# Narrow experts: fewer background steps, the decode last, half sums in other tiles; branch hints moved and added; the last expert's third block turned earlier

## The chip, the core and the metric

The kernel runs on one core of a Trainium2 chip. The metric is the device time of the slowest core in microseconds (us); the kernel before takes 634.35 us (median of 3 runs, 633.63 to 634.43). TensorE (PE) multiplies, VectorE (DVE) and ScalarE (ACT) work on tiles, GpSimd (POOL) and SyncE (SP) issue transfers here. Each engine runs its own instructions in order and waits on semaphores of the others.

## What is computed

Three layers on 2 sequences of 768 tokens with 512 features: attention of 8 heads (8 global tokens and a window of 96), a layer of 8 experts, and a Fourier mixing with a channel network. The change is in the experts:

```python
for s in range(S):
    fresh_e = argmax(logits[b, s])
    e = fresh_e if s == 0 or local_gate[b, s] < 0.5 else prev_e
    prev_e = e
    h = np.maximum(x[b, s] @ w1[e], 0.0)     # 512 -> 1024
    out[b, s] = p[e] * (h @ w2[e])           # 1024 -> 512
```

Every token goes to one expert, by data. With these inputs the experts 0 to 7 have 324, 177, 166, 172, 115, 206, 96 and 280 tokens.

## The kernel before

After attention and routing, `Moe.run` takes the experts e0 to e7 one after the other (from 127 to 321 us of the profile), each in blocks of 128 tokens that are gathered by index. Products are made in pairs of a high and a low part of each fp32 operand, so that a product of 512 by 1024 is 12 matmuls for each half of 512 columns.

`expert` branches on the number of blocks. Experts with two blocks go through `wide()`: `first256` for the first product (four quarters of 24 matmuls, each into one of two buffers of `ps_h`, read by `hh` on ScalarE and `hl` on VectorE), `third()`, which is a branch on n > 2, and `result` for the second product of each block. An expert with one block goes through `narrow()`: `first128` makes the first product with the tokens stationary, in two half sums; each is copied to SBUF (L1259), turned back by four transposes into `xtp` (L1243), and split into `hh` (L1245, ScalarE) and `hl` (L1246, VectorE). e4 and e6 are narrow here, e1, e2, e3 and e5 wide with `third` skipped. The last expert, e7, is done by sequence: a first block, the third block (taken here), then the second; inside its third block stands a further branch, `rest`, for more than three blocks (not taken here).

Beside the matmuls runs a background of generators. `bg.step(n)` advances each of them n times; `first128` and `second` call the step after every third matmul; `bg.drain()` runs them to the end. The order in which these calls come is the order of the instructions on ScalarE and VectorE. The background of expert e has three things. It converts the four weight pieces of expert e+1 (`Ring.take` on "e"): each is 1024 KB in one of four raw buffers, cast in two halves by ScalarE (L1048, tiles `wide`, `sl0h`, `sl1h`, `sl5h`) with its low parts by VectorE (L1050); when the piece is done, the load of the piece four places on is issued on SP's queue (L986). In experts 0 to 5 it decodes one or two pieces of the later layer ("d": L1081 on ScalarE, then L1090 to L1096 on VectorE, in a tile "dec" of which there are two; the result is written out by POOL, L1014). And `tokens(e + 1)` turns and splits the next expert's tokens (L1164, L1167, L1168). In narrow experts a "dec" tile also holds each half sum.

`mark_branch_hint_location` (L1344) puts a hint for TensorE ahead of the branch of the next expert.

Of the kernel before, what the change touches and what calls it, by code (L numbers as in the profile page):

```python
# [11 lines left out]
F32 = mybir.dt.float32  # L12
# [11 lines left out]
P = 128  # L24
B, H, S, D = 2, 8, 768, 64
E, F = 8, 1024
DM = H * D
# [9 lines left out]
LAST = E - 1  # L37
# [635 lines left out]
TOKENS = 4  # L673
# [253 lines left out]
def rows(st, g):  # L927

    n = 2 if g % 4 < 2 else 4
    out = []  # L930
    for j in range(2):
        hi, lo = (t.rearrange("p (k n) -> p k n", k=n) for t in st.ring.get("e", g + j))
        out += [(hi[:, k], lo[:, k]) for k in range(n)]
    return out
# [165 lines left out]
class Moe:  # L1100
# [81 lines left out]
    def write(self, y, p, d, name="more", beside=None):  # L1182

        nc = self.tc.nc
        ys = self.work.tile([P, DM], F32, name=name, bufs=2 if name == "ys" else 1)
        nc.scalar.activation(ys, y, AF.Copy, scale=p)
        self.scatter(ys, d, beside)
# [43 lines left out]
    def first128(self, w1, x, h, acc, turn, step=lambda: None, hs=None):  # L1231
# [8 lines left out]
        def turned(u):  # L1240
            tp = turn[0].tile([P, 4, P], F32, name=turn[1])
            for k in range(4):
                T.transpose(tp[:, k], hs[u][:, k * P:(k + 1) * P], self.st.ident)  # L1243
            o = slice(4 * u, 4 * u + 4)
            A.activation(hh[:, o], tp, AF.Relu)  # L1245
            V.scalar_tensor_tensor(hl[:, o], tp, 0.0, hh[:, o].bitcast(F32), op0=ALU.max, op1=ALU.subtract)  # L1246
# [12 lines left out]
            A.copy(hs[u], ps)  # L1259
        return lambda: turned(1)  # L1260

    def expert(self, e, n, more, ahead=None):
        tc, ring = self.tc, self.st.ring
        pc, ent = self.pc[e % 2], self.ent[e % 4]
        w1, w2 = rows(self.st, 4 * e), rows(self.st, 4 * e + 2)
        bg = Background()

        def chain(*gs):
            for g in gs:
                yield from g  # L1270


        at = 0 if e else 1
        step = lambda: bg.step(2)
        spare = self.ps_more, "more"

        def result(c, h, y, ys, *more):
            y = self.second(*h, w2, *y, *more)
            bg.drain()
            last = e == LAST and c == 1  # L1280
            write = lambda: self.write(y, pc[:, c:c + 1], ent[:, c, 1:2], ys, "first" if last else None)
            if last:
                self.finish = write
            else:
                write()

        def third():
            self.weight(e, (2,))

            with tc.If(n > 2):  # L1290
                for _ in self.turn(2, 0, self.place(e, 2)):
                    pass
                if e == LAST:
                    self.rest(more)
                late = self.first128(w1, *self.more, spare, spare)
                result(2, self.more[1], spare, "more", lambda: None, late)

        def pieces():
            for units in ring.plan[e]:
                for kind, m in units:  # L1300
                    if kind == "d":
                        ring.begun.pop(ring.at[kind, m], None)
            return ([ring.take(*u, follow=e < LAST) for u in units] for units in ring.plan[e])

        own = lambda s, c: [t[:, :, c * P:(c + 1) * P] for t in s]
        first, then = pieces()

        def wide():
            bg.add(chain(*first))
            calls = iter(range(8))  # L1310
            self.first256(e, lambda: bg.step(2) if e or next(calls) > 1 else None)
            bg.drain()
            if e:
                third()
            bg.add(self.tokens(e + 1))
            bg.add(chain(*then))
            hs = self.hh[0], self.hl[0]
            result(at, own(hs, 0), (self.ps_y, "y"), "ys", step)
            if e:
                result(1, own(hs, 1), spare, "more")  # L1320
            else:
                with tc.If(n > at + 1):
                    result(at + 1, own(hs, 1), spare, "more")

        def narrow():
            first, then = pieces()
            bg.add(chain(*first))
            h = own((self.hh[0], self.hl[0]), 0)
            late = self.first128(w1, own((self.xh[e % 2], self.xl[e % 2]), 0), h, (self.ps_h, "h"), (self.ps_x, "xtp"), step)
            bg.drain()  # L1330
            bg.add(chain(*then))
            calls = iter(range(8))

            def behind():
                if next(calls) == TOKENS:
                    bg.add(self.tokens(e + 1))
                bg.step(2)

            result(0, h, (self.ps_y, "y"), "ys", behind, late)

        if e < LAST:
            if e + 2 < E:
                self.entries(e + 2)
                tc.mark_branch_hint_location(f"wide{e + 1}", hint=(ahead > 1), engines=[mybir.EngineType.PE])  # L1344
            if e == 0:
                wide()
                return
            with tc.If(n > 1, label=f"wide{e}") as arm:
                wide()
            with arm.Else():  # L1350
                narrow()
            return

        for c in range(2):
            x, h = (own(s, c) for s in ((self.xh[e % 2], self.xl[e % 2]), (self.hh[0], self.hl[0])))
            late = self.first128(w1, x, h, (self.ps_h, "h"), (self.ps_x, "xtp"), step, [x[:, :DM] for x in self.xg[:2]])
            if c == 0:
                third()
                bg.add(chain(*first))
            result(c, h, (self.ps_y, "y"), "ys", step, late)  # L1360
            if c == 0:
                self.fetch(0)
# [9 lines left out]
    def rest(self, more):  # L1372

        tc, st, io = self.tc, self.st, self.io
        nc = tc.nc
        A, V = nc.scalar, nc.vector

        def fetch(e, j):
            for u in range(2):
                hi, lo = st.ring.get("e", 4 * (LAST - 1) + 2 + u)  # L1380
                for c in range(0, PW, 1024):
                    cs = slice(c, c + 1024)
                    t = self.st.ring.work.tile([P, PW // 2], F32, name="dec")
                    nc.sync.dma_start(t, io["we"][bass.ds(e * 4 + j + u, 1), :, cs].rearrange("o p n -> (o p) n"))
                    A.copy(hi[:, cs], t)
                    V.tensor_tensor(lo[:, cs], t, hi[:, cs].bitcast(F32), op=ALU.subtract)

        def rows(n):
            out = []
            for u in range(2):  # L1390
                hi, lo = (t.rearrange("p (k n) -> p k n", k=n) for t in st.ring.get("e", 4 * (LAST - 1) + 2 + u))
                out += [(hi[:, k], lo[:, k]) for k in range(n)]
            return out

        with tc.If(more > 0):
            x = self.place(LAST - 1, 2)

            with tc.For_i(0, E + 1, 1) as i:
                n = nc.values_load(st.nch[0:1, bass.ds(i, 1)], min_val=0, max_val=NC)
                e = nc.s_assert_within(i - (i >> 3), 0, LAST, skip_runtime_bounds_check_because="8 becomes 7, the others stay")  # L1400
                first = e * LIST + (i >> 3) * S - ((e + 1) >> 3) * (P + P // 2) + 1
                with tc.For_i(L3, NC, 1) as c:
                    with tc.If(n > c):
                        row = nc.s_assert_within(first + c * P, 0, E * LIST, skip_runtime_bounds_check_because="the row is in the list")
                        p = self.work.tile([P, 1], F32, name="p")
                        o = self.work.tile([P, 2], I32, name="o")
                        nc.sync.dma_start(o, st.list[bass.ds(row, P)])
                        self.gather(x, st.xs, o[:, 0:1])
                        V.tensor_copy(p, x[:, bass.ds(e + DM, 1)])
                        fetch(e, 0)  # L1410
                        s = (LAST - 1) % 2
                        for _ in self.turn(s, 0, x):
                            pass
                        self.first128(rows(2), (self.xh[s][:, :, :P], self.xl[s][:, :, :P]), self.more[1], (self.ps_more, "more"), (self.ps_more, "more"))()
                        fetch(e, 2)
                        y = self.second(*self.more[1], rows(4), self.ps_more, "more")
                        self.write(y, p, o[:, 1:2])
# [522 lines left out]
```

## Time and profile before

| | |
|---|---|
| median of 3 runs | 634.35 us |
| the profiled execution | 635.4 us |
| its span in the profile | 633.6 us |
| TensorE busy | 609.5 us (96%) |
| VectorE, ScalarE, GpSimd busy | 383.8, 275.3, 100.5 us |
| mean granted clock of TensorE | 0.992 |

Times below are us from the start of the span. A row of a timeline gives start, length, engine, line and operation, output and input, shape, count, and in brackets the idle time before it with what released it. The granted clock is TensorE's, as a share of full speed.

### The profile page before, as it was taken

The numbers are of one execution on the slowest core, as the hardware profiler recorded it, in microseconds if no ns is written. First come the engines' busy times: TensorE is split into PE (matmuls) and PEld (weight loads), VectorE is DVE, ScalarE is ACT, GpSimd is POOL, SyncE is SP. The second block draws the span as 40 slices with busy tenths as digits, with TensorE's granted clock in tenths as the row PEclk, the third lists the DMA queues.
The fourth block names the chain that finished last, engine by engine and source line by source line (L and its number), as shares of the span: only waits on it lengthen the run. The fifth ranks groups of instructions, "written<-read, shape, count | busy, mean of one in ns | idle before, by whom it ended". The sixth has DMA issues, their size and how long they took to land.

```text
span 633.6 us, 9722 instructions
## 1 busy us (share of the span) xinstructions
PE 609.5 (96%) x3506; PEld 494.1 (78%) x3507; DVE 383.8 (61%) x898; ACT 275.3 (43%) x548; POOL 100.5 (16%) x147
## 2 busy tenths in 40 slices
PE   9999998799999969898999999999999999999997
PEld 4777875499899849687867887888888888888885
DVE  5778786279786968661389987997531221272112
ACT  5789883266475556552434533441121221131010
POOL 2146662315313312300100000000000000000000
PEclk9999999999999989989999999999999999999999
DMA  8568762279978989961260242551100100100001
GB/s 278 187 204 203 201 120 68 49 283 337 372 250 278 335 288 327 339 210 66 87 250 32 95 173 92 187 190 63 67 0 1 32 36 0 67 2 0 1 0 66
DMA packets 25192, 92.49 MB, mean 146 GB/s; under 512 B 7645, under 2 KB 8797, under 8 KB 17185
## 3 DMA queue, kind: packets, MB, share of 16 engines
q1 hardware_dynamic: 19664, 79.50, 37.6%
q0 software_dynamic: 4736, 10.56, 4.6%
q10 hardware_dynamic: 720, 1.55, 0.7%
q8 instruction: 36, 0.59, 0.4%
q14 instruction: 36, 0.29, 0.2%
HBM read 81.00 MB, written 14.84 MB: 151 GB/s over the span
## 4 chain that ended last, share of the span: by engine, by line
PE 52%; DVE 1%; ACT 0%; issue 0%; DVEq 0%; ACTq 0%
PE h L1742 21%; PE acc L1757 7%; PE acc L1756 7%; PE acc L1758 7%; PE y L1204 1%; PE acc L1576 1%; PE acc L1562 1%; PE more L1254 1%; PE h L1254 1%; PE more L1204 1%; PE f L1708 1%; PE f L1605 1%; PE h L50 1%; PE f L1627 0%; DVE u L1767 0%; PE acc L1565 0%
## 5 line engine op out<-in xcount | busy, mean ns | idle before, releaser
L1747 DVE SCALAR_TENSOR_TENSOR hl<-h,hh 128x512 fp32r<-128x512 f32 x48 | 33.1, 689 | 117.5 <-ACT hh L1746 117.5
L1746 ACT ACTIVATE hh<-h 128x512 fp32r<-128x512 f32 x48 | 28.8, 600 | 164.3 <-PE h L1742 164.3
L1050 DVE TENSOR_TENSOR wide<-raws,wide 128x1024 fp32r<-128x1024 f32 (+1 forms) x38 | 44.8, 1201 | 24.4 <-ACT wide L1048 24.4
L168 ACT ACTIVATE t<-t,nm 128x256 f32<-128x256 f32 (+1 forms) x96 | 46.0, 480 | 10.7 <-DVE nm L159 9.9
L1742 PE MATMUL h<-un0h,wide 128*128 128x512 f32 (+1 forms) x136 | 42.4, 378 | 0.1
L1048 ACT CAST wide<-raws 128x1024 fp32r<-128x1024 f32 (+2 forms) x42 | 40.6, 993 | 4.1 <-PE acc L1758 3.4
L159 DVE CUSTOM_DVE_ANT_0 t<-sp,bias 128x256 f32<-128x256 f32 (+1 forms) x96 | 32.8, 398 | 8.3 <-PE sp L150 4.4
L1757 PE MATMUL acc<-wide,hh 128*128 128x512 f32 x96 | 37.8, 393 | 0.0
L1756 PE MATMUL acc<-wide,hh 128*128 128x512 f32 x96 | 37.6, 392 | 0.0
L1758 PE MATMUL acc<-wide,hl 128*128 128x512 f32 x96 | 37.5, 390 | 0.0
L1133 POOL DMA_INDIRECT xg<-xs,ent x23 | 28.7, 1250 | 39.9 <-PE y L1204 17.4
L1742 PEld LDWEIGHTS h<-un0h,wide 128*128 128x128 f32 x136 | 25.0, 188 | 5.0 <-ACT un0h L1517 0.3
L178 PE MATMUL tp<-consts,t 128*128 128x128 f32 x176 | 26.1, 283 | 1.7 <-ACT p L184 1.7
L178 PEld LDWEIGHTS tp<-consts,t 128*128 128x128 f32 x176 | 18.9, 141 | 9.3 <-ACT p L184 4.9
L1742 PE MATMUL h<-un0l,wide 128*128 128x512 f32 (+1 forms) x68 | 25.6, 377 | 0.0
L192 PE MATMUL sm<-p,vs 128*64 128x128 f32 x352 | 24.5, 279 | 0.0
L184 ACT COPY p<-tp 128x512 f32<-128x512 f32 (+1 forms) x48 | 24.3, 537 | 0.3 <-PE tp L178 0.3
L1081 ACT ACTIVATE dec<-raws 128x1024 f32<-128x1024 f32 x18 | 20.6, 1143 | 4.8 <-issue 4.8
L1224 PE MATMUL h<-xh,wide 128*128 128x256 f32 x160 | 22.5, 279 | 0.0
L1096 DVE SCALAR_TENSOR_TENSOR dec<-raws,dec 128x1024 int32<-128x1024 int32 x18 | 22.0, 1225 | 0.6
L1094 DVE SCALAR_TENSOR_TENSOR dec<-raws,dec 128x1024 int32<-128x1024 int32 x18 | 22.0, 1222 | 0.4
L192 PEld LDWEIGHTS sm<-p,vs 128*64 128x64 f32 x352 | 18.7, 136 | 3.8 <-issue 3.8
(474 smaller groups left out, 1602.3 us busy)
## 6 DMA issues: line engine op xcount, KB each, us to landing
raws<-we SPq DMA_DIRECT2D x31, 1024.0 KB
raws<-wm SPq DMA_DIRECT2D x18, 1024.0 KB
raws<-wmf SPq DMA_DIRECT2D x7, 1024.0 KB
wmf<-dec POOLq DMA_DIRECT2D x8, 512.0 KB
xs<-xrow SPq DMA_DIRECT2D x12, 260.0 KB
vs<-v SPq DMA_DIRECT2D x6, 512.0 KB
raws<-kq SPq DMA_DIRECT2D x3, 1024.0 KB
u<-x SPq DMA_DIRECT2D x6, 512.0 KB
```

The costliest lines, as they stand in the source:

```text
L159: V.tensor_tensor_reduce(out=u.t[:, x, :u.W], in0=u.sp[:, j, k, :u.W], in1=bias[:, 4 * u.g + x, u.b0:u.b0 + u.W], scale=-0.125, scalar=3.0 ...
L168: A.activation(u.t[:, x, :u.W], u.t[:, x, :u.W], AF.Exp, bias=u.nm[:, x:x + 1], scale=-1.0, accum_out=u.den[:, x])
L178: T.transpose(u.tp[k][:, j, c], u.t[:, 2 * k + j, c * P:(c + 1) * P], st.ident)
L192: T.matmul(turned[j * D:j * D + D, k], vs[:, ti % KS, u.h + 2 * k + j], u.p[:, 2 * k + j, c], start=c == 0, stop=c == len(tiles) - 1)
L1048: (first or nc.scalar.copy)(hi[:, cs], raw[:, cs])
L1050: (eng() if callable(eng) else eng or nc.vector).tensor_tensor(lo[:, cs], raw[:, cs], hi[:, cs].bitcast(F32), op=ALU.subtract)
L1742: nc.tensor.matmul(ps[:, c], a[:, k], x[:, k, c], start=n == 0, stop=n == 11)
L1746: nc.scalar.activation(hh, ps, AF.Relu)
L1747: nc.vector.scalar_tensor_tensor(hl, ps, 0.0, hh.bitcast(F32), op0=ALU.max, op1=ALU.subtract)
L1756: T.matmul(acc[c], hh[:, cs], h2, start=first, stop=False)
L1757: T.matmul(acc[c], hh[:, cs], l2, start=False, stop=False)
L1758: T.matmul(acc[c], hl[:, cs], h2, start=False, stop=last)
```

## The change

In `narrow`, a call of the step advances the background once, not twice; in the first product only the first two weight pieces are in it, in the second the other two, until after some steps `tokens(e + 1)` takes their place; what is left of them and the decode come after the result. The half sums go into the tile of the unused third block (`xg2` in e4 and e6) and into a tile `ys`. The hint of the next expert moves from the start of `expert` into `tell()`: after the first block's result in `wide`, after the first product in `narrow`. New hints stand for `third` at the start of `wide` and of e7, and for `rest` in e7's third block. In e7 the third block's tokens are turned in the background of the first block's first product, and `rest` moves behind the third block's result.

```diff
--- before.py
+++ after.py
@@ -1259,6 +1259,9 @@
             A.copy(hs[u], ps)
         return lambda: turned(1)
 
+    def hint(self, label, stay):
+        self.tc.mark_branch_hint_location(label, hint=stay, engines=[mybir.EngineType.PE])
+
     def expert(self, e, n, more, ahead=None):
         tc, ring = self.tc, self.st.ring
         pc, ent = self.pc[e % 2], self.ent[e % 4]
@@ -1287,13 +1290,16 @@
         def third():
             self.weight(e, (2,))
 
-            with tc.If(n > 2):
-                for _ in self.turn(2, 0, self.place(e, 2)):
-                    pass
+            with tc.If(n > 2, label=f"third{e}"):
+                if e < LAST:
+                    for _ in self.turn(2, 0, self.place(e, 2)):
+                        pass
+                else:
+                    self.hint("rest", more > 0)
+                late = self.first128(w1, *self.more, spare, spare)
+                result(2, self.more[1], spare, "more", lambda: None, late)
                 if e == LAST:
                     self.rest(more)
-                late = self.first128(w1, *self.more, spare, spare)
-                result(2, self.more[1], spare, "more", lambda: None, late)
 
         def pieces():
             for units in ring.plan[e]:
@@ -1305,7 +1311,13 @@
         own = lambda s, c: [t[:, :, c * P:(c + 1) * P] for t in s]
         first, then = pieces()
 
+        def tell():
+            if e + 2 < E:
+                self.hint(f"wide{e + 1}", ahead > 1)
+
         def wide():
+            if e:
+                self.hint(f"third{e}", n > 2)
             bg.add(chain(*first))
             calls = iter(range(8))
             self.first256(e, lambda: bg.step(2) if e or next(calls) > 1 else None)
@@ -1316,6 +1328,7 @@
             bg.add(chain(*then))
             hs = self.hh[0], self.hl[0]
             result(at, own(hs, 0), (self.ps_y, "y"), "ys", step)
+            tell()
             if e:
                 result(1, own(hs, 1), spare, "more")
             else:
@@ -1323,25 +1336,36 @@
                     result(at + 1, own(hs, 1), spare, "more")
 
         def narrow():
-            first, then = pieces()
-            bg.add(chain(*first))
+            units = [u for part in ring.plan[e] for u in part]
+            for u in units:
+                if u[0] == "d":
+                    ring.begun.pop(ring.at[u], None)
+            takes = {u: ring.take(*u) for u in units}
+            d = [takes[u] for u in units if u[0] == "d"]
+            bg.add(chain(*(takes["e", 4 * e + 4 + k] for k in range(2))))
             h = own((self.hh[0], self.hl[0]), 0)
-            late = self.first128(w1, own((self.xh[e % 2], self.xl[e % 2]), 0), h, (self.ps_h, "h"), (self.ps_x, "xtp"), step)
+            late = self.first128(w1, own((self.xh[e % 2], self.xl[e % 2]), 0), h, (self.ps_h, "h"), (self.ps_x, "xtp"), bg.step,
+                                 [self.place(e, 2)[:, :DM], self.work.tile([P, DM], F32, name="ys", bufs=2)])
             bg.drain()
-            bg.add(chain(*then))
+            tell()
+            then = chain(*(takes["e", 4 * e + 6 + k] for k in range(2)))
+            bg.add(then)
             calls = iter(range(8))
 
             def behind():
-                if next(calls) == TOKENS:
+                k = next(calls)
+                if k == TOKENS:
+                    bg.live.remove(then)
                     bg.add(self.tokens(e + 1))
-                bg.step(2)
+                bg.step()
 
             result(0, h, (self.ps_y, "y"), "ys", behind, late)
+            bg.add(chain(then, *d))
+            bg.drain()
 
         if e < LAST:
             if e + 2 < E:
                 self.entries(e + 2)
-                tc.mark_branch_hint_location(f"wide{e + 1}", hint=(ahead > 1), engines=[mybir.EngineType.PE])
             if e == 0:
                 wide()
                 return
@@ -1351,6 +1375,8 @@
                 narrow()
             return
 
+        self.hint(f"third{e}", n > 2)
+        bg.add(self.turn(2, 0, self.place(e, 2)))
         for c in range(2):
             x, h = (own(s, c) for s in ((self.xh[e % 2], self.xl[e % 2]), (self.hh[0], self.hl[0])))
             late = self.first128(w1, x, h, (self.ps_h, "h"), (self.ps_x, "xtp"), step, [x[:, :DM] for x in self.xg[:2]])
@@ -1392,7 +1418,7 @@
                 out += [(hi[:, k], lo[:, k]) for k in range(n)]
             return out
 
-        with tc.If(more > 0):
+        with tc.If(more > 0, label="rest"):
             x = self.place(LAST - 1, 2)
 
             with tc.For_i(0, E + 1, 1) as i:
```

Where it moves instructions, before and after. On ScalarE, in e4 from its first product on, before (`raws` is a loaded piece, `h` a half sum in PSUM, `dec` a decode tile):

```order
L1048 CAST wide_106<-raws_63 128x1024 x4
L1259 COPY dec_8489<-h_8490 128x512
L1081 ACTIVATE dec_8518<-raws_63 128x1024
L1245 ACTIVATE hh256_6327<-xtp_8525 128x4x128
L1259 COPY dec_8489<-h_8513 128x512
```

And after:

```order
L1048 CAST wide_106<-raws_63 128x1024 x2
L1259 COPY xg2_6353<-h_8523 128x512
L1048 CAST wide_106<-raws_63 128x1024
L1245 ACTIVATE hh256_6327<-xtp_8550 128x4x128
L1048 CAST wide_106<-raws_63 128x1024
L1259 COPY ys_8522<-h_8541 128x512
```

Two casts stand ahead of the first copy instead of four, and the decode's start (L1081) is gone from between the copy and `hh`.

On VectorE, from the end of e4 into e5, before (the branch is that between the two experts):

```order
L1050 TENSOR_TENSOR sl5l_6319<-raws_63,sl5h_6318 128x1024 x2
L1168 TENSOR_TENSOR xl1_6349<-xtp_8576,xh1_6346 128x4x128
L1168 TENSOR_TENSOR xl1_6349<-xtp_8586,xh1_6346 128x4x128
L1180 COPY pc_6331<-xg0_6351 128x1
L1180 COPY pc_6331<-xg1_6352 128x1
L1348 UNCONDITIONAL_BRANCH
L1348 REGISTER_ALU x2
L1348 COMPARE_AND_BRANCH
L1050 TENSOR_TENSOR sl0l_103<-raws_63,sl0h_102 128x1024
L1228 SCALAR_TENSOR_TENSOR hl256_6329<-h_8647,hh256_6327 128x512
```

And after:

```order
L1050 TENSOR_TENSOR sl5l_6319<-raws_63,sl5h_6318 128x1024 x2
L1090 TENSOR_SCALAR dec_8647<-dec_8647 128x1024
L1092 TENSOR_SCALAR dec_8647<-dec_8647 128x1024
L1094 SCALAR_TENSOR_TENSOR dec_8647<-raws_63,dec_8647 128x1024
L1096 SCALAR_TENSOR_TENSOR dec_8647<-raws_63,dec_8647 128x1024
L1372 UNCONDITIONAL_BRANCH
L1372 REGISTER_ALU x2
L1372 COMPARE_AND_BRANCH
L1050 TENSOR_TENSOR sl0l_103<-raws_63,sl0h_102 128x1024
L1228 SCALAR_TENSOR_TENSOR hl256_6329<-h_8687,hh256_6327 128x512
L1050 TENSOR_TENSOR sl0l_103<-raws_63,sl0h_102 128x1024
L1050 TENSOR_TENSOR sl1l_105<-raws_63,sl1h_104 128x1024
```

The low parts of the last piece and the decode stand between the tokens of e5 and its first `hl` (L1228); before, the decode was done in the middle of e4.

On TensorE, around e7's third block, before:

```order
L1290 REGISTER_ALU
L1290 COMPARE_AND_BRANCH
L1164 MATMUL more_9579<-consts_66,xg3_6354 128x128 x4
L1395 REGISTER_ALU
L1395 COMPARE_AND_BRANCH
```

And after, in the first block's first product:

```order
L1254 MATMUL h_9590<-wide_106,xh1_6346 128x512 x3
L1164 MATMUL more_9594<-consts_66,xg3_6354 128x128 x4
L1254 MATMUL h_9590<-wide_106,xh1_6346 128x512
L1254 MATMUL h_9590<-sl5h_6318,xh1_6346 128x512
L1254 MATMUL h_9590<-sl5l_6319,xh1_6346 128x512
```

The four transposes of the third block's tokens now stand between the first matmuls of the first block, and the branch `rest` no longer follows them.

## Rows read from the trace of the kernel before

**Rows 1.** Waits of TensorE, 127 to 330: us in total, times, longest

```profile
PE y L1204 <- ACT hh L1245: 4.3, 1, 4.3
PE h L1254 <- ACT wide L1048: 2.0, 1, 2.0
PE more L1254 <- DVEq L1395: 1.6, 1, 1.6
```

**Rows 2.** Timeline of TensorE, e4: start, length, instruction, [idle before <- releaser]

```profile
220.58 1.09 PE L1254 MATMUL h<-wide,xh 128*128 128x512 f32 x4
...
226.10 0.66 PE L1243 MATMUL xtp<-consts,dec 128*128 128x128 f32 x4 [1.16 <-ACT dec L1259]
...
232.45 0.79 PE L1204 MATMUL y<-sl0h,hh 128*128 128x512 f32 x1 [4.30 <-ACT hh L1245]
...
242.30 1.10 PE L1224 MATMUL h<-xh,wide 128*128 128x256 f32 x8
243.24 0.63 PE L1224 MATMUL h<-xl,wide 128*128 128x256 f32 x4
```

**Rows 3.** Timeline of ScalarE, e4

```profile
221.66 3.90 ACT L1048 CAST wide<-raws 128x1024 fp32r<-128x1024 f32 x4
...
230.80 1.12 ACT L1081 ACTIVATE dec<-raws 128x1024 f32<-128x1024 f32 x1 [4.75 <-issue]
```

**Rows 4.** Two stretches: busy by engine, granted clock, DMA share, GB/s

```profile
232.00:240.00 8.00, 7.55 (x24) 6.06 (x25) 7.93 (x9) 5.28 (x8) 0.58 (x1) 0.58 0.57 180
268.00:274.00 6.00, 6.00 (x21) 4.74 (x22) 4.54 (x4) 3.26 (x4) 0.00 (x0) 0.72 0.85 284
```

**Rows 5.** Timeline of TensorE, e5's middle to e7's start

```profile
253.04 0.63 PE L1224 MATMUL h<-xl,wide 128*128 128x256 f32 x4
253.81 0.93 PE L1204 MATMUL y<-wide,hh 128*128 128x512 f32 x3
...
264.82 1.07 PE L1204 MATMUL more<-sl5h,hl 128*128 128x512 f32 x4
267.92 0.47 PE L1254 MATMUL h<-sl0h,xh 128*128 128x512 f32 x1 [2.03 <-ACT wide L1048]
...
282.44 1.10 PE L1254 MATMUL h<-wide,xh 128*128 128x512 f32 x4
```

**Rows 6.** Transfers by queue, 264 to 268

```profile
q8 instruction: 1, 0.02, 1.5%
```

**Rows 7.** Timeline of VectorE, 231 to 256

```profile
231.94 0.69 DVE L1090 TENSOR_SCALAR dec<-dec 128x1024 f32<-128x1024 f32 x1 [4.51 <-ACT dec L1081]
...
235.13 1.22 DVE L1096 SCALAR_TENSOR_TENSOR dec<-raws,dec 128x1024 int32<-128x1024 int32 x1
...
239.14 2.36 DVE L1050 TENSOR_TENSOR sl5l<-raws,sl5h 128x1024 fp32r<-128x1024 f32 x2
...
245.98 0.69 DVE L1228 SCALAR_TENSOR_TENSOR hl<-h,hh 128x512 fp32r<-128x512 f32 x1 [0.60 <-ACT hh L1227]
```

**Rows 8.** Timeline of ScalarE, end of e4

```profile
237.33 2.00 ACT L1048 CAST sl5h<-raws 128x1024 fp32r<-128x1024 f32 x2
...
242.50 0.69 ACT L1186 ACTIVATE ys<-y,pc 128x512 f32<-128x512 f32 x1 [0.81 <-PE y L1204]
```

**Rows 9.** Issue of one load, and the stretch after it

```profile
236.42 0.33 SPq L986 DMA_DIRECT2D raws<-we  x1
...
236.40:241.20 4.80, 4.80 (x22) 3.85 (x21) 4.80 (x5) 3.62 (x6) 0.58 (x1) 0.76 0.78 207
```

**Rows 10.** Timeline of TensorE and VectorE, e7's third block

```profile
288.47 0.60 PE L1164 MATMUL more<-consts,xg 128*128 128x128 f32 x4
...
289.78 0.69 DVE L1168 TENSOR_TENSOR xl<-more,xh 128x512 fp32r<-128x512 f32 x1 [1.07 <-ACTq L1395]
...
290.67 0.70 PE L1254 MATMUL more<-wide,xh 128*128 128x512 f32 x2 [1.60 <-DVEq L1395]
```

## The prediction

> **What bounds the kernel.** The list of what TensorE waited for comes first: it is busy for 609.5 of 633.6 us, and over all the experts and the start of the mixing four waits are worth naming, 4.3, 2.0 and 1.6 us [rows 1] and 1.16 [rows 2], 9.1 us together. All four lie where the change is: two in e4, one at the start of e6, one in e7's third block. The rest is matrix work that the change leaves alone, so the gain is these four, and what the clock lost after them, less what takes their place.
>
> TensorE's timeline of e4 shows two of them [rows 2]: 1.16 at 226.10, behind the copy of the first half sum, and 4.30 at 232.45, behind an hh. ScalarE's timeline of the same stretch says why [rows 3]: four casts of background (3.90 us from 221.66) stand ahead of that copy, and ahead of the hh stands the start of a decode, L1081, which itself idled 4.75 us for its buffer: it is one of the two "dec" tiles, and the older one was still on its way out. ScalarE works in order, so hh waited for a decode that nobody in e4 needed. After the 4.30 the granted clock fell: the 8 us from 232 have a mean of 0.58 [rows 4].
>
> e6 starts 2.03 late [rows 5]: e5's last four matmuls at 264.82 are over near 265.7, the next is at 267.92. The row names an ACT cast; but e6's first product reads weights and tokens that were ready long before, and the transfers of 264 to 268 hold one packet of queue q8, which carries instructions [rows 6]. I read it as TensorE waiting for its code after the jump to the narrow arm. The clock then has a mean of 0.72 over 268 to 274 [rows 4].
>
> **e4.** It takes 242.30 - 220.58 = 21.72 us now [rows 2]. What it takes undisturbed comes from e6, the same narrow program: 282.44 - 267.92 = 14.52 [rows 5], of which 6 x (1 - 0.72) = 1.7 is clock [rows 4], so 12.9. The same way e4 is 21.72 - 1.16 - 4.30 - 8 x 0.42 (3.4) = 12.9. In the changed order two casts instead of four stand ahead of the copy: 221.66 + 1.95 = 223.6, and the half sum is complete near 223.6 too, so the copy ends about 224.2; its transposes were due at 226.10 - 1.16 = 224.94. No wait. The decode's start stands behind the result, and half sums no longer need a "dec" tile. The piece that is cast ahead of the second hh has its load issued at 220.88, so I leave 0.2 for a cast that waits a little. e4: 13.1, a gain of 8.6, and nothing of the clock is lost. Bounds: 6 to 8.8.
>
> **e5 pays much of it back.** This is what I did not find in the diff but in VectorE's order. What e4 no longer does beside its matmuls, it does after them: two low parts of the last piece and the four decode instructions now stand ahead of e5's first own work on VectorE. Let E be e5's start. ScalarE writes e4's result (0.69) and casts (2.00 for two, the first done after some 1.05) [rows 8]: E + 1.8. VectorE's two low parts take 2.36 [rows 7]: E + 4.15. The decode ran from 231.94 to 235.13 + 1.22 = 236.35 with one hl of about 0.6 between [rows 7], so 3.8 alone: E + 7.95. Then comes one low part, sl0l, half of the 2.36 and a little, 1.23, and only then the hl of e5's first quarter, 0.69: E + 9.95, with the branch E + 10.0. first256 ends at 253.04 + 4 x 0.1175 = 253.51 (eight matmuls took 243.24 - 242.30) [rows 2, 5], so a quarter of it takes (253.51 - 242.30) / 4 = 2.80. The third quarter writes into the buffer that this hl reads, as there are two; it is due at E + 5.6 and starts at E + 10.1: a stop of 4.5. In the kernel before, that hl was at 245.98, 3.7 after e5's start, and nothing waited.
>
> The fourth quarter waits for the second hl, and ahead of that stand, on ScalarE and VectorE, the cast and the low part of the next piece. Its raw buffer is the one that the decode held: the load is issued only after the decode, at E + 8.0 (before: at 236.42, six us ahead of e5 [rows 9]). That load was alone: by 241.2 the queues had moved 4.8 x 207 = 994 KB, so 4.8 us for its 1024 KB [rows 9]. It lands at E + 12.8; cast 1.05, low part 1.22, hl 0.69: E + 15.8. The third quarter ended at E + 12.9, so a stop of 3.0. After E + 15.9 come the fourth quarter and the 12.2 us from 253.51 to 265.7: e5 takes 30.9 instead of 23.4, a loss of 7.5. What follows the stops in clock: 0 to 1.7 each by [rows 4]; while the next stop follows within 3 us a slow clock is hidden in it, so only the last counts, and I take 0.4. Bounds: 0, as in the e5 of before, to 16, worked out below.
>
> **e6.** The same order of casts, and no decode in e6. The narrow arm itself shows no wait behind its casts in e6, and from the due 265.72 (264.82 and four matmuls) it takes 282.44 - 265.72 = 16.7 where 12.9 would do: 2.1 of stop and 1.7 of clock, 3.8. The hint for the narrow arm is moved from the start of e5 to the middle of its second half, about 6 us ahead of the jump instead of 23. At the other boundaries the early hint leaves no gap; here code passed in between. I take it that the stop goes; it is the least sure term: 0 to 3.8. Its start, the end of e5, moves to 220.58 + 13.1 + 30.9 + 0.4 = 265.0; e7 starts at 278, 4.5 earlier.
>
> The Trainium skill ("Runtime: NRT & Kernel Launch", section "Instruction fetch mechanics") says that a taken branch to a target outside the two blocks that an engine holds must fetch before it goes on. The trace agrees in part: one stop of 2.03 with an instruction packet beside it, but none at the other expert boundaries. By that rule the stop stays and the sum would be 631.
>
> **e7.** The third block's tokens are turned and cast inside the block: transposes at 288.47, low part at 289.78, next product at 290.67, idle 1.60 [rows 10]. Now they are turned in the first chunk's steps, whose VectorE is all but idle there. The four transposes move, they don't go. The `rest` branch, not taken, is moved behind the block: such a branch costs TensorE what a skipped third block does, 253.81 - 253.51 = 0.3 [rows 5]. Gain 1.60 + 0.2 - 0.3 = 1.5. The new hints ahead of skipped third blocks: that 0.3 is a drain that stays, so nothing (bounds -0.3 to +1.2 over four experts).
>
> **Sum.** -8.6 + 7.5 + 0.4 - 3.8 - 1.5 = -6.0. The profiled execution took 635.4 (span 633.6), 1.05 above the median of 634.35; taken off the median it is 628.3.
>
> **Rivals.**
> - *The stop before e6 stays.* For it: the jump is the same, and the row shows no cause in the data. Against: five boundaries without a gap. e6 then gains 0 (clock falls too) to 1.5: 630.6 to 632.1. Chance 0.27.
> - *e5 pays back little.* If the decode didn't stand ahead of the hl, this would come at E + 6.2 and the load 3.8 earlier: 0.7 and 3.0, so 3.7; without any stop, 0. Against: two buffers and an engine that works in order. The time is 620.5 to 624.5. Chance 0.10.
> - *e5 pays back more than e4 gave: slower.* Place: the load of e5's second cast piece. It stands in the queue behind another 1024 KB load issued at E + 4.2 and beside the decoded 512 KB and the gathers. If it takes 10 us rather than 4.8, the fourth quarter starts 5.2 later, after a stop of 8 that carries 3.4 of clock as the 4.30 did. e5 costs 16, e6 gains nothing: -8.6 + 16 - 1.5 = +6, 640. It decides from a cost of 11.4 in e5 on. For it: the DMA share is 0.57 and 0.85 over the two long stretches of [rows 4], so there is other traffic; against: the load alone needed 4.8. Chance 0.09.
> - *Nothing is left of it.* e5 costs 8.6 to 11, the stop before e6 stays: 633 to 635.6. This is the change that only moves the wait. Chance 0.09.
>
> **Numbers.** Forecast 0.45. A measurement of this kernel tells 0.2% (1.3 us) from no change. Faster: 0.45 + 0.27 + 0.10 and a little of the last = 0.83; within: 0.08; slower: 0.09. The range 624.3 to 633.9 leaves out most of the second and third rival and half of the last. The likeliest alone: 626.5 to 630.5.
>
> **What would show it.** In the profile after: no wait of y or xtp in e4, e4 near 13 us, no low clock in it; e5 of 30 to 31 us with two stops in its first half, released by VectorE's hl, the second with a load behind it; e6 starting near 265 without a stop; no wait in e7's third block. I am wrong if e5 shows no stops (then near 621), or if one of them exceeds 6 us (then slower).

## The result: slower by 1.4%, and the profile after

The changed kernel takes 641.90 us (median of 4 runs, 641.45 to 642.85), the kernel before 633.99 beside it (631.16 to 634.43): a ratio of 1.0136 with an interval of 1.0104 to 1.0169. The forecast was 628.3 with a range of 624.3 to 633.9. It was wrong in sign.

The profiled execution took 642.26, its span is 640.5 against 633.6, so 6.9 us are to be found. TensorE's first matmul of each stage gives the stages; e6, and e4 in the changed kernel, are counted from the moment they were due, the end of the matmuls of the expert before:

| stage | before | after | difference | forecast |
|---|---|---|---|---|
| e4 | 21.72 | 16.75 | -5.0 | -8.6 |
| e5 | 23.42 | 35.22 | +11.8 | +7.9 |
| e6 | 16.72 | 17.19 | +0.5 | -3.8 |
| e7 | 38.56 | 37.62 | -0.9 | -1.5 |
| all the rest | | | +0.5 | 0 |

The waits of TensorE from 127 to 330, as in [rows 1] (us in total, times, longest), have other names:

```profile
PE h L1224 <- DVE hl L1228: 7.7, 2, 5.9
PE h L1254 <- ACT wide L1048: 2.5, 1, 2.5
PE h L1254 <- issue: 2.4, 1, 2.4
PE h L1224 <- DVE sl5l L1050: 1.8, 1, 1.8
PE xtp L1243 <- ACT xg L1259: 0.9, 1, 0.9
PE y L1204 <- PEq L1421: 0.6, 1, 0.6
```

The y wait of 4.3 and e7's 1.6 are gone, as foreseen. The 2.0 at e6's start stayed as 2.5. In place of the rest stand VectorE's hl, a wait for sl5l and two waits in e4 (2.4 at its start, 0.9 behind the copy) that weren't foreseen. TensorE's timeline shows where they lie:

```profile
223.01 1.16 PE L1254 MATMUL h<-wide,xh 128*128 128x512 f32 x4 [2.38 <-issue]
...
228.32 0.66 PE L1243 MATMUL xtp<-consts,xg 128*128 128x128 f32 x4 [0.88 <-ACT xg L1259]
...
237.22 1.20 PE L1224 MATMUL h<-xh,wide 128*128 128x256 f32 x8
240.27 0.74 PE L1224 MATMUL h<-xl,wide 128*128 128x256 f32 x4 [1.84 <-DVE sl5l L1050]
...
247.03 1.20 PE L1224 MATMUL h<-xh,wide 128*128 128x256 f32 x8 [1.82 <-DVE hl L1228]
...
255.95 2.07 PE L1224 MATMUL h<-xh,wide 128*128 128x256 f32 x8 [5.86 <-DVE hl L1228]
...
271.53 1.07 PE L1204 MATMUL more<-sl5h,hl 128*128 128x512 f32 x4
275.12 0.47 PE L1254 MATMUL h<-sl0h,xh 128*128 128x512 f32 x1 [2.52 <-ACT wide L1048]
```

e4 begins at 223.01 and not at 220.47, when e3 was through; e5 has three stops in its first half, 9.5 us together. VectorE over the same stretch:

```profile
241.31 0.68 DVE L1090 TENSOR_SCALAR dec<-dec 128x1024 f32<-128x1024 f32 x1
...
244.01 1.23 DVE L1096 SCALAR_TENSOR_TENSOR dec<-raws,dec 128x1024 int32<-128x1024 int32 x1
245.16 1.22 DVE L1050 TENSOR_TENSOR sl0l<-raws,sl0h 128x1024 fp32r<-128x1024 f32 x1
246.29 0.68 DVE L1228 SCALAR_TENSOR_TENSOR hl<-h,hh 128x512 fp32r<-128x512 f32 x1
...
254.07 1.23 DVE L1050 TENSOR_TENSOR sl1l<-raws,sl1h 128x1024 fp32r<-128x1024 f32 x1 [5.96 <-ACT sl1h L1048]
255.21 0.68 DVE L1228 SCALAR_TENSOR_TENSOR hl<-h,hh 128x512 fp32r<-128x512 f32 x1
```

The decode ends at 245.24, the first hl comes at 246.29, and TensorE's 247.03 follows it. That is the chain of the prediction: 9.8 us after e5's start, against 10.1 forecast. The second hl is late because of a cast on ScalarE:

```profile
220.72 0.69 ACT L1186 ACTIVATE more<-more,pc 128x512 f32<-128x512 f32 x1 [4.80 <-PE more L1204]
225.79 2.00 ACT L1048 CAST wide<-raws 128x1024 fp32r<-128x1024 f32 x2 [4.38 <-DMA raws<-wm]
227.69 0.58 ACT L1259 COPY xg<-h 128x512 f32<-128x512 f32 x1
...
252.99 1.04 ACT L1048 CAST sl1h<-raws 128x1024 fp32r<-128x1024 f32 x1 [8.96 <-DMA raws<-we]
```

The cast of sl1h at 252.99 waited for a load. On SP's queue that load is the one of 245.31, issued when the decode had let go of its raw buffer; the one of 217.06, of a piece "wm", is what the cast at 225.79 waited for, told of below:

```profile
217.06 0.33 SPq L990 DMA_DIRECT2D raws<-wm  x1
...
245.31 0.33 SPq L986 DMA_DIRECT2D raws<-we  x1
```

It took 252.99 - 245.31 = 7.7 us. In [rows 9] a load took 4.8. What the queues moved from 245.3 to 253 (packets, MB, share; q1 carries the loads, q0 the gathers and the decoded piece):

```profile
q1 hardware_dynamic: 639, 1.52, 65.9%
q0 software_dynamic: 300, 0.75, 25.4%
```

Stretches of the changed kernel (columns as in [rows 4]):

```profile
245.30:253.00 7.70, 3.06 (x24) 2.86 (x24) 2.81 (x3) 0.01 (x1) 0.59 (x1) 0.94 0.91 294
254.00:258.00 4.00, 2.05 (x9) 2.05 (x10) 3.90 (x5) 2.98 (x5) 0.00 (x0) 0.50 0.14 59
258.00:260.00 2.00, 2.00 (x16) 2.00 (x15) 2.00 (x3) 0.00 (x0) 0.00 (x0) 0.76 1.02 299
274.00:280.00 6.00, 4.88 (x14) 3.91 (x15) 2.36 (x2) 1.72 (x3) 0.66 (x1) 0.72 0.82 309
```

The queues weren't slow: they moved 7.7 x 294 KB = 2.26 MB, while one load is 1024 KB (1.05 MB). It shared them with the decoded 512 KB, gathers and a part of the next load, issued at 248.87. The load issued 3.9 us earlier was hardly in its way: q1 moved 1.02 MB from 241.4 to 245.3, nearly all of it. In the 4.8 us of [rows 9] q0 moved 0.00 MB, so there no gathers and no decoded piece went beside the load. After the stop of 5.86 the clock was at 0.50 for 4 us, the lower level of the two, and 0.76 for 2 more.

### The profile page after: what moved, and what is told of

Its sections match the earlier page's. It is cut to its first block, busy times and chain, and to the rows that moved or that the text cites. A ratio compares the mean times of both kernels' runs of the same rounds, so it can differ in the third digit from the quotient of the medians.

```text
span 640.5 us, 9743 instructions
## 1 busy us (share of the span) xinstructions
PE 609.3 (95%) x3506; PEld 493.5 (77%) x3507; DVE 384.1 (60%) x898; ACT 274.6 (43%) x548; POOL 99.7 (16%) x147
## 4 chain that ended last, share of the span: by engine, by line
PE 50%; DVE 1%; issue 0%; ACT 0%; DVEq 0%; ACTq 0%
PE h L1768 21%; PE acc L1783 7%; PE acc L1782 7%; PE acc L1784 7%; PE y L1204 1%; PE acc L1602 1%; PE acc L1588 1%; PE h L1254 1%; PE f L1734 1%; PE f L1631 1%; PE h L50 1%; PE f L1653 0%; DVE u L1793 0%; PE acc L1591 0%; PE f L1634 0%; PE acc L1653 0%
## 5 line engine op out<-in xcount | busy, mean ns | idle before, releaser
L1224 PE MATMUL h<-xh,wide 128*128 128x256 f32 x160 | 23.9, 289 | 7.7 <-DVE hl L1228 7.7
L1224 PEld LDWEIGHTS h<-xh,wide 128*128 128x128 f32 x160 | 21.5, 197 | 8.7 <-DVE hl L1228 8.1
L192 PEld LDWEIGHTS sm<-p,vs 128*64 128x64 f32 x352 | 18.7, 136 | 3.8 <-issue 3.6
```

The lines of the kernel that those rows point to most:

```text
L192: T.matmul(turned[j * D:j * D + D, k], vs[:, ti % KS, u.h + 2 * k + j], u.p[:, 2 * k + j, c], start=c == 0, stop=c == len(tiles) - 1)
L1224: T.matmul(ps[:, u], w[:, f], x[:, k], start=n == 0, stop=n == 11)
```

## The experiments

"Hints" below are TensorE's branch hints: the one for the next expert, which the change moves, and those for `third` and `rest`, which it adds. Two theories stood against each other at first. One: what e4 put off, the decode above all, stands in e5's way, and its cost was only sized too low. The other: the hints. A third came from the traces: a difference in the order in which the two arms of a branch take the pieces. All ratios are to the kernel before, run beside it; "the best version" is e5_ring_order. In every profile e6 starts 0.7 to 3.7 us late.

**Hints back.** The changed kernel with the hints of the kernel before (`tell()` and the hints for `third` and `rest` out, `mark_branch_hint_location` at the start of `expert` again).

> The changed kernel with the hints of the kernel before: one hint per expert, at its start; none for third and rest. Theory A (the late hint causes the stop of 2.4 us at e4's start): that stop goes, the stop of 2.5 at e6's start stays as in both kernels, and e5's three stops stay, as they come from VectorE's order and the load behind it. e5 then starts about 2.4 earlier, the total falls from 641.9 to 639.5. Rival B (the longer code of narrow, or where it lies, causes the stop at e4): the stop stays, 641.9. Rival C (hints had nothing to do with it, the first cast's wait for the decode's load holds up e4): TensorE starts e4 on time but then waits some 3.3 us for the first copy instead of 0.9, 641.5.

642.99 (641.01 to 646.95), ratio 1.0161 (1.0093 to 1.0229): no gain that shows, though with four runs so far apart one of 2 us could hide. e4 starts without a gap, but its first cast still comes at 226.64, and xtp waits 2.18 for the copy behind it, where the changed kernel has 2.38 and 0.88. So one wait had been hidden behind another. e5's third stop stays at 5.84.

**Hints only.** The kernel before with the change's hints.

> The kernel before with only the hints of the change. Theory A (late hint): a stop of about 2.4 us stands at e4's start, as in the changed kernel; most of it is hidden, since TensorE then waits for hh behind the decode's start until about 232.4 anyway, so that wait shrinks from 4.3 to about 2 and the total is 634 to 635. Rival B (layout of narrow's code): no stop at e4's start, 634. A gain at the skipped third blocks would show as gaps below 0.3 us there, at most 1.2 us together, 633.

637.15 (634.01 to 638.57), ratio 1.0057 (1.0029 to 1.0084): slower by 3.5 us, where 634 to 635 was expected. So the hints cost something, and hints back shows that this isn't what holds e5.

**No decode in e4.** The changed kernel with e4's decode given to e5.

```diff
-            for _ in range(-(-min(e + 1, E - 2) * 2 * EARLY // (E - 2)) + -min(e, E - 2) * 2 * EARLY // (E - 2)):
+            for _ in range((2, 1, 1, 2, 0, 2, 0)[e]):
                 (a if len(a) == 2 else b).append(next(d))
```

> The changed kernel, but the plan gives e4 no decode: expert 5 decodes two pieces instead of one. Theory A (the decode at e4's end delays e5's first hl on VectorE by 3.8 us and the load behind it by 8): e5's stops of 1.8, 1.8 and 5.9 shrink to one of about 1 or less and its low clock goes, e5 takes 24 to 25 us instead of 35.2; the stops at e4's and e6's start stay. Total 641.9 - 10.5 = 631.4. Rival B (e5 lacks data because the loads as such are too slow after a short e4): the stops move to another piece and the gain is below 5, 637 or more.

633.23 (630.82 to 637.32), ratio 0.9983 (0.9951 to 1.0016): 8.7 us less than the changed kernel's 641.90 (two comparisons, each beside the kernel before). VectorE's order at e5's start, with no decode in it:

```profile
242.39 1.21 DVE L1050 TENSOR_TENSOR sl0l<-raws,sl0h 128x1024 fp32r<-128x1024 f32 x1
243.53 0.68 DVE L1228 SCALAR_TENSOR_TENSOR hl<-h,hh 128x512 fp32r<-128x512 f32 x1
...
246.40 0.68 DVE L1228 SCALAR_TENSOR_TENSOR hl<-h,hh 128x512 fp32r<-128x512 f32 x1
```

e5 starts at 238.31, so the first hl comes at +5.2, and none of the three stops is left (the longest gap there is 0.3). The first theory is shown: the decode and what stood behind it held e5. But e4's first cast still waited for a load, 4.16 us.

**Early hints and no decode in e4.**

> The two together: hints as before, and no decode in e4. Theory A: the gains add, 641.9 - 10.5 - 2.4 = 629.0, faster than the kernel before by about 5 us: e4 about 14 instead of 21.7, e5 about 24.5, e6 unchanged, e7 0.9 less. Rival B (what is saved ahead is lost behind it to loads): 634.

632.29 (631.39 to 635.29), ratio 0.9968 (0.9941 to 0.9995). e4 is still 17.6 long, with one wait of 3.06 behind the copy. Its first cast:

```profile
226.07 1.99 ACT L1048 CAST wide<-raws 128x1024 fp32r<-128x1024 f32 x2 [3.96 <-DMA raws<-we]
```

and the three loads ahead of it on SP's queue, one after the other at 215.25, 217.57 and 221.46:

```profile
215.25 6.54 SPq L986 DMA_DIRECT2D raws<-we  x3
```

In [rows 3] the same cast came at 221.66, behind a load of 220.88, at once: the piece that it reads had long been there. In the program the cast waits for one load before the change and for two after it. The changed narrow arm puts the decode last and the wide arm doesn't, so the two arms of an expert issue the same loads in different order. In the wide arm of e3 the piece that e4 casts first comes by the arm's third load, in the narrow arm by its fifth. Behind the branch the cast waits for both. e3 took the wide arm here, where the fifth load is another piece's: the one of 217.57 (in the changed kernel the "wm" of 217.06, which the cast's row names). The cast came 8.5 us after its issue, in the changed kernel 225.79 - 217.06 = 8.7. The next run tests whether this is what e4 lost.

**Ring order in both arms.** The same, with narrow's pieces taken in the plan's order:

```diff
...
-            takes = {u: ring.take(*u) for u in units}
-            d = [takes[u] for u in units if u[0] == "d"]
-            bg.add(chain(*(takes["e", 4 * e + 4 + k] for k in range(2))))
+            first, then = pieces()
+            bg.add(chain(*first))
...
-            then = chain(*(takes["e", 4 * e + 6 + k] for k in range(2)))
+            then = chain(*then)
...
-            bg.add(chain(then, *d))
+            bg.add(then)
```

> As the kernel with the early hints and no decode in e4 (632.3, e4 17.6 us with a wait of 3.06 for the first copy), but the narrow arm converts its pieces in the order of the ring again, as the wide arm does. With these inputs e4 and e6 then have the same instructions in the same order; only the arms that are not taken differ. Theory A: in the change the two arms of an expert issue their loads in another order, so behind the branch a piece can have come by either of two loads, and the first cast of the next expert waits for both, the later one being that of a piece needed much later. With one order the first cast waits for its own load alone: it starts near 221.7 instead of 226, the wait of 3.06 and the low clock behind it go, e4 takes 13 to 13.5. Total 632.3 - 4 = 628.3. Rival B: the first cast waits for its own load, late for the queues' sake: no change, 632.3.

627.64 (625.01 to 633.82), ratio 0.9894 (0.9863 to 0.9925): 4.7 us less than without the equal order (in another comparison), and better than both kernels. In its program the cast waits for one load again. The cast, in a second profile of this version (e11_ring_again):

```profile
221.34 0.69 ACT L1186 ACTIVATE more<-more,pc 128x512 f32<-128x512 f32 x1 [4.80 <-DMA xg<-xs,ent]
222.16 1.05 ACT L1048 CAST wide<-raws 128x1024 fp32r<-128x1024 f32 x1
```

222.16 is 4.7 us after the issue of the load that would be the second, at 217.50, and the cast doesn't wait. e4 takes 13.06 there.

**Decode last in both arms.** The changed kernel with its decode kept in e4 and put last in the wide arm too: in the plan only `b.append(next(d))`.

> The changed kernel with its hints, but the plan puts the decode last in every expert, in both arms, so the ring's order is that of the narrow arm: the load of the second piece of e6's first product no longer waits for the decode in e4, and both arms issue their loads alike. The decode stays between e4's result and e5's first hl. Theory A (three causes: order of VectorE, the load behind the decode, two orders of loads): e5's third stop of 5.9 and the low clock behind it go, the first cast of e4 starts on time; left are the stop of 2.4 at e4's start (hint), about 4.3 at e5's third quarter, and e6's. Total 641.9 - 5.9 - 1.5 - 0.9 + 0.6 = 634. Rival B (VectorE's order is the whole cause in e5): the third stop stays, 641.

633.40 (632.09 to 637.59), ratio 0.999 (0.9969 to 1.0012). The first cast doesn't wait, and in e5 the third stop is gone and the first two have become one. A stop of 1.39 stands in e4 instead, behind a later cast that waits for its load. What is left in e5, on TensorE:

```profile
247.21 2.08 PE L1224 MATMUL h<-xh,wide 128*128 128x256 f32 x8 [3.87 <-DVE hl L1228]
```

and on ScalarE:

```profile
244.50 1.04 ACT L1048 CAST sl1h<-raws 128x1024 fp32r<-128x1024 f32 x1 [0.34 <-DMA raws<-we]
```

sl1h comes at 244.50, since its load is no longer behind the decode. The two parts of the prediction's e5 term are told apart: the decode ahead of hl alone stops TensorE by 3.87, the load issued behind the decode made the third stop.

**Hints in the middle**, one run: the best version with the next expert's hint after its first product.

> The kernel of the ring's order, with each hint moved from the start of its expert to the middle (between the two products). Theory A (a hint too near to its jump or on the wrong side of a stretch of code gives a stop): e6's stop of 2 to 2.6 changes, either gone (626) or joined by one at e4's start (630). Rival B (e6's stop has nothing to do with hints): both as with the early hint.

627.44; no gap at e4's start.

**e7's part alone**, in the kernel before.

> The kernel before with only the last expert's part: the third block's tokens turned in the first block's product, the branch rest behind the third block's result, no hints. Prediction's step: the wait of 1.6 goes, 0.3 comes back at the branch: 632.5 to 633. From the changed kernel's trace: 0.6 comes back at the branch, e7 0.9 shorter: 633. Rival: ScalarE or VectorE, now with more to do in the first block, hold up its half sums: 634.35.

632.36 (631.15 to 634.75), ratio 0.9974 (0.995 to 0.9997), 1.6 us, just clear of noise. Its profile, with the hints of before, surprised by e4's start:

```profile
226.44 2.04 PE L1254 MATMUL h<-wide,xh 128*128 128x512 f32 x4 [4.79 <-ACT wide L1048]
```

**Second profiles**, to see what of the gaps varies from one execution to the next: of the changed kernel,

> The changed kernel once more, for a second profile of it. Theory (what holds e5 is in the program: the decode and the second load stand ahead of its hl): the three stops of e5 come again, about 1.8, 1.8 and 5.9 us, and the time is 641 to 643. If the 2.38 at e4's start is a stop for code that falls differently from one execution to the next, it may be gone or another here (0 to 5 us); if it is the moved hint, it is 2.4 again. Rival (the profile of after was an odd one): the third stop of e5 is under 3 us and the time under 638.

of the kernel before,

> The kernel before once more. Theory: the wait of 4.3 behind hh in e4 and the 1.6 in e7 come again, since they follow from the order of ScalarE; e6's start is late again by 1 to 3 us; e4's start may be late here by some us although it was not in the first profile, if these stops vary by execution. Rival (a stop belongs to a program): e4's start has no gap, e6's has 2.0. Time 632 to 635.

and of the best version:

> The version with early hints, no decode in e4 and the pieces in ring order in both arms, once more (its profiled run had 3.9 us at e4's start and 1.8 at e6's, and took 632.8, while its timed runs had a median of 627.6). If those stops vary by execution, the 3.9 is smaller or gone here and the time is 625 to 629; if they belong to the program, 3.9 comes again and the time is 632 to 633.

The changed kernel again (644.72): e5's stops come again, 1.84, 1.84 and 6.56, and so does the gap at e4's start:

```profile
223.51 2.05 PE L1254 MATMUL h<-wide,xh 128*128 128x512 f32 x4 [2.75 <-issue]
```

The kernel before again (635.49): no gap at e4, 2.20 at e6, 3.66 behind hh. The best version again (625.71): no gap at e4, where its first profile had 3.90. So this gap varies by execution. Over all 18 profiles: with the change's hints it is 2.38, 2.75, 2.12, 1.88, 0.62 and, in the kernel before with these hints, none; with the added hints alone 2.76; with the moved hint alone or the hint in the middle three times none; with the hints of before 3.90, 4.79 and six times none.

**The best version with the change's hints.**

> The same version (no decode in e4, pieces in ring order in both arms) with the hints where the change put them. Theory that the place of the hints costs little once e5 is free: 627 to 629, ratio to before 0.989 to 0.992. Rival that the change's hints cost by themselves what they cost when put alone into the kernel before (3.5 us): 631, ratio 0.995.

630.76 (627.98 to 632.61), ratio 0.9951 (0.9933 to 0.9969): the rival of the expectation, 3 us more than the best version. Its interval lies clear of the one above (0.9863 to 0.9925) and overlaps the one below (0.9896 to 0.9958). A gap of 1.88 at e4's start again. Which of the hints it is, was tried on one chip with the best version beside them: the moved hint alone,

> The best version (early hints, no decode in e4, ring order in both arms; 627.6, ratio 0.9894), with only the hint of the next expert moved late, as the change moves it. If the 3.1 us between the versions with early and late hints are the moved hint, this takes 630 to 631 (ratio about 0.995) and its profile has a gap of some 2 us at e4's start; if they are the added hints, it takes 627 to 628 (0.989).

627.53 (625.00 to 628.22), ratio 0.9919 (0.9901 to 0.9937). The added hints alone:

```diff
         def wide():
+            if e:
+                self.hint(f"third{e}", n > 2)
```

(and those for e7's third block and for rest)

> The best version with only the added hints (for the third blocks and for rest), the next expert's hint early as before. If the added hints cost the 3.1 us, 630 to 631 (0.995); if the moved hint does, 627 to 628 (0.989). If each carries a part, both this and the moved hint alone lie near 629.

637.12 (634.62 to 641.11), ratio 1.0065 (1.0042 to 1.0088): more than either expectation. The best version itself:

> The best version itself on the same chip as the two above: 627.6 again (626 to 629), ratio 0.989. If it comes out at 630 or more, the 3.1 us between it and the version with late hints were the difference of two jobs and not of the hints.

627.91 (624.41 to 633.50), ratio 0.9927 (0.9896 to 0.9958). And the hint in the middle, timed:

> The best version with the next expert's hint in the middle of the expert (after its first product), timed. If the cost comes with how late the hint stands, this lies between early (627.6) and late (630 or more), about 628 to 629; if a hint at any distance is as good while it doesn't stand close ahead of the branch, 627.5.

627.81 (626.71 to 629.43), ratio 0.9922 (0.9898 to 0.9946). The place of the next expert's hint, early, middle or late, makes no difference that shows, as long as the added hints are out. The added hints cost 637.12 - 627.91 = 9.2 us beside the early hint, and some 3 beside the moved one. So the two act together. In the version of 637.12 the hint for the third block follows a few instructions behind the one for the next expert, before either of the branches that they are for; whether it takes that one's place is a rival that no run tries. TensorE with the added hints alone:

```profile
212.71 0.50 PE L1204 MATMUL y<-wide,hh 128*128 128x512 f32 x1 [1.69 <-issue]
...
225.98 1.91 PE L1254 MATMUL h<-wide,xh 128*128 128x512 f32 x4 [2.76 <-ACT wide L1048]
...
268.43 0.77 PE L1254 MATMUL h<-sl0h,xh 128*128 128x512 f32 x1 [3.68 <-ACT wide L1048]
```

Three gaps: in the middle of e3's second product, which goes on 3.5 us behind its skipped third block, at e4's start and at e6's; the best version's profiles have the last alone, with the exception named above. Together they are 8.1 us, 5.5 more than the one of 2.62 in the profile of the best version beside it; the rest of the 9.2 isn't traced. "issue" says that the first of them waited for nothing in the data. That TensorE waits for its code there is my reading; no run shows the fetch itself.

## Why the prediction was wrong

**e4, forecast -8.6, came -5.0.** The step that failed is "the copy ends about 224.2 ... No wait". The wait of 4.30 went. The copy's 1.16 stayed as 0.88, since the first cast waited for a second load, until 225.79, and with it the copy. Ahead of that the start itself was 2.5 late, where the hints had been priced at nothing. That this gap comes of the hints is likely, by the 18 profiles above, and not shown for one execution. The two overlap, so hints back alone gained nothing that shows. That e4 undisturbed takes 13 was right: 13.06 in the second profile of the best version.

**e5, forecast +7.9, came +11.8.** The mechanism was right: the third quarter started at +9.8 (forecast 10.1; the terms of hl's +9.95 add to 9.87), and without the decode the stops went. The term that was mis-sized is the load, "That load was alone ... so 4.8 us". It took 7.7, so the fourth quarter came at +18.7 instead of +15.9: 2.8. The remaining 1.1 is clock: from 255.95 to e5's end are 16.5 us instead of 15.0, after the stop of 5.86, and 0.4 of it had been allowed for. This is the place that the third rival named, with the 512 KB and the gathers in the queue; the load ahead, which it named too, had nearly landed. It was given 0.09. The 4.8 was from a stretch in which the gathers and the decode moved 0.00 MB; alone it wasn't quite, as a second load was issued at 239.25 in that stretch. The stop ahead of the third quarter was forecast at 4.5; 1.82 of it came there, and 1.84 already on the first xl matmul, which waited for sl5l, a tile that it doesn't read. That is the order of the two arms again. In the program the matmul waits until VectorE has done a number of instructions, one number for both arms of e4. In the wide arm xl is ready at the 1271st of the count, in the narrow arm at the 1268th, and the number is 1271, in the narrow arm the first half of sl5l. With the decode last in both arms it is 1268, and there the two stops are the one of 3.87.

**e6, forecast -3.8, came +0.5.** "I take it that the stop goes" failed, and the first rival holds: 2.52 late, and 0.72 of clock over 274 to 280 as in [rows 4]. The rule of the Trainium skill ("Runtime: NRT & Kernel Launch", section "Instruction fetch mechanics"), by which a taken branch to a target out of its window fetches first, fits e6's start, late in all 18 profiles. It fits e4's start, the same kind of jump, less well: ten profiles have no gap there. The instruction packet of [rows 6] doesn't tell them apart, as the kernel before and the best version have one from 219 to 222 too, beside an e4 that starts on time. With early, middle and late hints the gap is there (2.6, 2.4 and 2.0 on one chip), so the place of the hint doesn't set it; what does stays open.

**e7, forecast -1.5, came -0.9 in the profile and -1.6 timed alone.** The 1.60 of [rows 10] is gone, and `rest`, which was put at 0.3, takes 0.60. On TensorE in the changed kernel, at the third block's first matmul and behind that block:

```profile
295.63 0.62 PE L1254 MATMUL h<-sl5h,xl 128*128 128x512 f32 x2
296.09 1.10 PE L1254 MATMUL more<-wide,xh 128*128 128x512 f32 x4
...
308.82 0.50 PE L1204 MATMUL y<-sl0h,hh 128*128 128x512 f32 x1 [0.60 <-PEq L1421]
```

**The sum.** Forecast -6.0 us, in the profile +6.9, 12.9 apart: e4 3.6, e5 3.9, e6 4.3, e7 0.6, the rest 0.5. No term came out better than forecast. Those of e4 (8.6 out of 6 to 8.8) and e6 (3.8 out of 0 to 3.8) had been taken at their good ends, and the load's bad end stood only in a rival.

## What to carry to other kernels

Work that is taken out of one stage's shadow has to be put where the next stage's first product doesn't stand behind it on an in-order engine, and the load that waits for its buffer moves with it; price that load with what is in the queue at its new time, not by the row of a load that had them nearly to itself. When two arms of a branch share a ring of buffers, issue the loads in the same order in both, or the code behind the branch waits for both. When several waits overlap at one place, removing one can show nothing: take them out one by one and together.

## What the runs showed of the hardware

- The hints for the third blocks, of which four are skipped and one is taken, and for rest cost 9.2 us together beside the early hint for the next expert (637.12 against 627.91), and 3.5 in the kernel before beside the moved one. The gaps seen stand away from the branches that they are for. The hint for the jump to the next expert alone costs nothing that shows, early or late.
- The gap at the entry of a narrow expert varies from one execution to the next: at e4's start 3.90, 0 and 0 in three profiles of the best version, 4.79 with e7's part alone.
- The granted clock doesn't fall after every gap. In the changed kernel it was 0.72 over the 6 us around e6's start, after a gap of 2.52; in the second profile of the best version it stayed at full over the 6 us around the same gap of 2.52:

```profile
258.00:264.00 6.00, 3.48 (x16) 2.68 (x15) 3.35 (x3) 2.84 (x4) 4.19 (x4) 1.00 0.98 391
```
